# Causal mask added by TensorE for all 32 pairs of heads, in an attention plus SwiGLU kernel

## The chip, the cores and the metric

One NeuronCore of a Trainium2 chip runs the whole program. The metric is the device time of one execution, in microseconds (us); lower is better. PE is TensorE, DVE is VectorE, ACT is ScalarE, POOL is GpSimd, SP is SyncE, which here only issues DMAs.

## The reference, cut to what matters

```python
def _attn_ref(q, k, v, f):                       # q, k, v: 8 x 8 x 576 x 64; f: 8 x 8 x 576
    scores = scale * np.matmul(q, k.transpose(0, 1, 3, 2))
    cum = np.cumsum(np.log(np.clip(f, 0.0001, 1.0)), axis=-1)
    decay = cum[:, :, :, None] - cum[:, :, None, :]
    causal = np.triu(np.ones((S, S), dtype=bool), k=1)
    scores = np.where(causal, -1000000000.0, scores + decay)
    scores = scores - np.max(scores, axis=-1, keepdims=True)
    attn = np.exp(scores)
    attn = attn / (np.sum(attn, axis=-1, keepdims=True) + 1e-09)
    return np.matmul(attn, v)

def _moe_ref(x, w_gate, w_val, w_out):           # x: 4608 x 512; d_ff 1536
    g = x @ w_gate
    silu = g * (1.0 / (1.0 + np.exp(-g)))
    return silu * (x @ w_val) @ w_out
```

The attention output, with its heads side by side, is the input x of the second function. The gate sum of the query's own row drops out of the softmax, so the kernel needs only the sum of the key, as something that is added along a row of scores.

## The kernel before, in words

**Pairs.** Two heads make a pair p (0 to 31): 64 queries of one head and 64 of the other fill the 128 partitions. A pair has nine blocks of queries, i = 0 to 8, each with 64(i + 1) keys. They are worked in two units, g = 0 (blocks 0 to 3) and g = 1 (blocks 4 to 8), written a10.0, a10.1 and so on where the code names units.

**One unit.** `prepare` casts q and k to bf16 on POOL, transposes them on PE (L447) and copies them out (L459, L461). `scores` multiplies them on PE into a bank `sp` of PSUM (L493); there are two such banks for all pairs, and `BANKS` lists which blocks share one. DVE then adds the gate sums `cb` to the scores, writes the sum to a tile `t` in SBUF and takes the row's least value into a small tile `tm`, all in one instruction with a second one that stores the least value (L517, twice in the trace: a custom operation and a READ_ACCUMULATOR). The scores have their sign turned, so the least value is the softmax's maximum. ACT takes the exponential (L532), `normalize` makes the reciprocals of the row sums (`lr`, L546 to L550) and multiplies on POOL (L568); then P is transposed, on PE for pairs 0 to 7 (L598), by one DMA a pair for pairs 8 to 31 (L581). `weighted` multiplies P with v on PE (L624), and the result goes to `xT`, a ring of 2560 tokens (L648).

**The causal mask.** Only the last 64 keys of a block, its diagonal, need a mask. There are two ways, chosen by `MFROM = 12`. For pairs 0 to 11, PE adds the mask: a second matmul of 64 columns, identity times mask, accumulates into the diagonal's columns of the bank (L497). For pairs 12 to 31, `copies` makes a tile `cm` a pair, the gate sums with the mask added, on POOL or DVE (L476), and `scores` cuts the DVE instruction of a block in two: one for the keys before the diagonal, with `cb`, and one for the 64 of the diagonal, with `cm`. The second takes the least value of the first as its start:

```python
                if last and a < QB * i and p >= MFROM:
                    cuts += [(i, a, QB * i), (i, QB * i, z)]
```

**The feed-forward part.** `gate` and `project` work on tiles of 128 to 512 tokens: two matmuls to `gv` (L706), tanh on ACT (L712), two DVE products (L714, L717), then the output matmul (L734), a copy out (L741, L743) and a DMA (L746).

**The order.** Every operation is handed to a planner (`Plan`) with a cost for each engine that may do it, a latency `lat` after it, and a priority `prio`. The planner lays the operations out in time by these numbers, takes the one that can start earliest, and so fixes, before the program runs, which engine does what and in which order. Attention has the lower priority numbers and goes first; feed-forward work fills what is left. On the chip each engine runs its instructions in that fixed order and waits by semaphores. `NUDGE` is a list of additions to the priorities of single units (a: attention, f: gate, o: project, q: prepare); `HEAD` is the order of the units of pairs 0 to 3.

Of the kernel before, what the change touches and what calls it, by code (L numbers as in the profile page):

```python
# [8 lines left out]
F32 = mybir.dt.float32  # L9
BF16 = mybir.dt.bfloat16  # L10
AF = mybir.ActivationFunctionType
ALU = mybir.AluOpType
# [2 lines left out]
BIG = 1.0e9  # L15
HUGE = 3.0e38
COLD = 25000


class Op:  # L20
# [11 lines left out]
class Plan:  # L32
# [29 lines left out]
    def order(self):  # L62
# [72 lines left out]
        while ready:  # L135
            best = None
            for n, r in ready.items():
                o = self.ops[n]
                got = room(o, r)
                if got is None:  # L140
                    continue
                for e, dur in o.engs.items():
                    s = max(r, got[0], free[e])
                    for k in o.reads:
                        if k in using and using[k][0] != e:
                            s = max(s, using[k][1])
                    c = (s + o.bias.get(e, 0), o.prio, n, e, dur, got[1])
                    if best is None or c[:4] < best[:4]:
                        best = c
            if best is None:  # L150
                raise RuntimeError("no operation can start: " + ", ".join(str(self.ops[n].writes) for n in list(ready)[:20]))
            s, _, n, e, dur, take = best
            o = self.ops[n]
            s -= o.bias.get(e, 0)
            if e == "PE" and s < COLD:
                dur *= 2
            for k, b in take:
                name = self.home[k]
                self.where[k] = b
                slots[name][b] = k  # L160
                taken[name, self.line[k]] += 1
            o.start, o.eng = s, e
            free[e] = s + dur
            for k in o.reads:
                if self.home.get(k) in self.banks:
                    using[k] = e, s + dur + 30
            if o.dma:
                q = e == "POOL"
                at = max(wire[q], s + (2550 if q else 2000))
                both = max(0, min(2 * o.dma, wire[not q] - at))  # L170
                wire[q] = at + o.dma + both / 2
                wire[not q] += both / 2
                if o.ring:
                    free[e] = max(free[e], wire[q] - 1450)
                o.end = wire[q] + 1100
            else:
                o.end = free[e] + o.lat
            for k in {*o.writes, *o.reads, *o.holds}:
                left[k] -= 1
                until[k] = max(until[k], o.end)  # L180
            del ready[n]
            for kid in kids.get(n, ()):
                waiting[kid.n] -= 1
                if not waiting[kid.n]:
                    ready[kid.n] = max(d.end for d in kid.deps)
            done.append(o)
# [10 lines left out]
def kernel(  # L197
# [12 lines left out]
    B, H, S, D = q.shape  # L210
# [3 lines left out]
    P = 128  # L214
# [19 lines left out]
             [[(8, 0, 512)], [(8, 512, 576), (6, 0, 448)], [(7, 0, 512)], [(5, 0, 384)], [(4, 0, 320)]]]  # L234


    MFROM = 12
    CMENG = ("POOL", "DVE")

    ON_PE = {(p, g) for p in range(8) for g in range(2)}  # L240

    NDIRECT = 0
    NSEL = 1
    MOST = (("p", 1), ("o", 2), ("f", 3))
# [11 lines left out]
    HEAD = "10 00 20 30 11 01 31 21"  # L256


    NUDGE = "a21.0:1 a31.1:10 f5:1 f7:4.5 o8:2 q11:-2 q15:4 q24:2.5"

    WAIT = ""
    ORDER = [(int(u[0]), int(u[1])) for u in HEAD.split()]
# [32 lines left out]
    for i in range(0, NB, 2):  # L295
        bufs(f"e{i}", [P, QB * (i + 2)], F32, 2)
    bufs("eo", [P, 512], F32, 4)
    bufs("tm", [P, NB + 1], F32, 6)
    bufs("ls", [P, NB, 2], F32, 6)
    bufs("lr", [P, NB], F32, 6)  # L300
    both = {}
    for n in ("pk", "pT"):
        both[n] = [sb.tile([P, sum(NSL), P], BF16, name=f"{n}{x}") for x in range(2)]
# [114 lines left out]
    def prepare(p):  # L418
        s = first[p]
        for name in ("k", "q"):  # L420
# [4 lines left out]
            def cast(e, name=name, fk=fk, bk=bk, KR=KR):  # L425
# [5 lines left out]
                    eng[e].tensor_scalar(dst, src, -scale, 1.0, op0=ALU.mult, op1=ALU.mult)  # L431
                else:
                    eng[e].tensor_copy(dst, src)
            engs = {"POOL": 850}
            if p < NPB:
                engs = {"POOL": 850, "ACT": 850, "DVE": 500} if name == "k" else {"POOL": 1050, "ACT": 1050, "DVE": 680}
            o = pl.op(engs, cast, [fk], [bk], s - 1 + (name == "q") * .1)
# [30 lines left out]
    def copies(p):  # L468

        if p < MFROM:  # L470
            return
        pl.key(("cm", p), "cm")

        def add(e):
            src = pl.buf(("cb", p)).rearrange("r (i c) -> r i c", c=QB)
            eng[e].tensor_tensor(pl.buf(("cm", p)), src, maskf.unsqueeze(1).to_broadcast((P, NB, QB)), op=ALU.add)  # L476
        cost = {"POOL": S * 1.05 + 245, "DVE": S / .96 + 82}
        pl.op({e: cost[e] for e in CMENG}, add, [(("cb", p), 3)], [("cm", p)], first[p] - .5, holds=[("cb", p)])

    def scores(p, g):  # L480
        s = at[p, g]
        pl.key(("tm", p, g), "tm")
        pl.key(("ls", p, g), "ls")
        for n, bank in enumerate(BANKS[g]):
            sk = ("sp", p, g, n)
            pl.key(sk, "sp")
            pr = s + n * .05

            def mult(e, bank=bank, sk=sk):
                sp, kt, qz, o = pl.buf(sk), pl.buf(("kt", p)), pl.buf(("qz", p)), 0  # L490
                for i, a, z in bank:
                    last = z == QB * (i + 1)
                    nc.tensor.matmul(sp[:, o:o + z - a], qz[:, i, :, :].rearrange("p h r -> p (h r)"), kt[:, a:z],  # L493
                                     start=True, stop=not last or p >= MFROM)
                    o += z - a
                    if last and p < MFROM:
                        nc.tensor.matmul(sp[:, o - QB:o], ident, mask, start=False, stop=True)  # L497
            cols = [z - a for _, a, z in bank] + [64 for i, a, z in bank if z == QB * (i + 1) and p < MFROM]
            pl.op({"PE": mm(*cols)}, mult, [("kt", p), ("qz", p), (("kt", p), "done"), (("qz", p), "done"), "mask"], [sk], pr, lat=220)
            o = 0  # L500
            cuts = []
            for i, a, z in bank:
                last = z == QB * (i + 1)
                if last and a < QB * i and p >= MFROM:
                    cuts += [(i, a, QB * i), (i, QB * i, z)]
                else:
                    cuts.append((i, a, z))
            for i, a, z in cuts:
                last = z == QB * (i + 1)
                own = last and p >= MFROM  # L510
                tk = ("t", p, i)
                if a == 0:
                    pl.key(tk, "t")

                def add(e, i=i, a=a, z=z, o=o, sk=sk, tk=tk, last=last, own=own):
                    tm = pl.buf(("tm", p, g))
                    nc.vector.tensor_tensor_reduce(  # L517
                        out=pl.buf(tk)[:, a:z], in0=pl.buf(sk)[:, o:o + z - a],
                        in1=pl.buf(("cm", p))[:, i, :] if own else pl.buf(("cb", p))[:, a:z], scale=1.0,
                        scalar=HUGE if a == 0 else tm[:, NB:NB + 1], op0=ALU.add, op1=ALU.min,  # L520
                        accum_out=tm[:, i:i + 1] if last else tm[:, NB:NB + 1])
                w = [tk, ("tm", p, g)] + ([("m", p, i)] if last else [("m", p, i, "part")])
                r = [sk] + ([("cm", p)] if own else [(("cb", p), 3)]) + ([("m", p, i, "part")] if a else [])
                pl.op({"DVE": (z - a) / .96 + (142 if a else 82)}, add, r, w, pr, lat=100, holds=[] if own else [("cb", p)])
                o += z - a
                if last:
                    ek = ("e", p, i)
                    pl.key(ek, epool(i))

                    def exp(e, i=i, tk=tk, ek=ek):  # L530
                        L = QB * (i + 1)
                        nc.scalar.activation(pl.buf(ek)[:, :L], pl.buf(tk)[:, :L], AF.Exp,  # L532
                                             bias=pl.buf(("tm", p, g))[:, i:i + 1], scale=-1.0,
                                             accum_out=pl.buf(("ls", p, g))[:, i, 0:1])
                    sums[p, g] = pl.op({"ACT": QB * (i + 1) * .833 + 290}, exp, [tk, ("m", p, i)], [ek, ("ls", p, g)],
                          pr, lat=150, holds=[("tm", p, g)])

    def normalize(p, g):
# [10 lines left out]
        pl.op({"DVE": 95, "ACT": 200}, guard, [("ls", p, g)] + ([("z", "ls", n) for n in range(6)] if p < 3 else []), [("lr", p, g)], s, lat=120)  # L549
        pl.op({"DVE": 95}, lambda e: nc.vector.reciprocal(lr(), lr()), [("lr", p, g)], [("l2", p, g)], s, lat=170, holds=[("lr", p, g)])  # L550
        kk = ("pk", p, g)
        joint = not any((p, x) in ON_PE for x in range(2))
        pl.key(kk, f"pk{g}", same=("pk", p, 1 - g) if joint else None)
        w = HI[g] - LO[g] + 1
        for i in range(HI[g], LO[g] - 1, -1):
# [75 lines left out]
    def spread(p, g, pv):  # L631
# [5 lines left out]
        for a, z in ((0, cut), (cut, w)):  # L637
# [3 lines left out]
            def evac(e, a=a, z=z):  # L641
# [5 lines left out]
                src = bass.AP(src.tensor, src.offset + QB * (z - a - 1), [full[0], [-QB, z - a], full[2]])  # L647
                (nc.scalar.copy if e == "ACT" else nc.vector.tensor_copy)(dst, src)  # L648
            tok = t0 + a * QB, t0 + z * QB
            o = pl.op({"ACT": QB * (z - a) * .833 + 130, "DVE": QB * (z - a) / .96 + 85}, evac, [xk],  # L650
                      [("x", hp, n) for n in range(tok[0] // QB, tok[1] // QB)], s)
            o.bias = LATER if p >= 8 else {}
            evacs.append((pv, tok))
# [1 line left out]
    def load_v(b):  # L655
        for c in range(5):
# [9 lines left out]
                (), [fk], s, dma=1460 if n == P else 800, after=wait)  # L666
            def cast(e, c=c, n=n, fk=fk):
                (nc.scalar.copy if e == "ACT" else eng[e].tensor_copy)(pl.buf(("vt", b))[0:n, c, :, :], pl.buf(fk)[0:n, :, :])
            o = pl.op({"POOL": 670} if b else {"POOL": 670, "ACT": 580, "DVE": 600}, cast,
                  [fk] + ([("z", "vt", b)] if c == 4 and b < 2 else []), [("vt", b), ("vt", b, c)], s + .5)  # L670
            o.bias = SPARE

# [183 lines left out]
```

## Time and profile before

| | |
|---|---|
| median of 3 runs | 425.94 us (425.29 to 428.68) |
| the profiled execution | 422.99 us, span 421.1 us |
| busy: PE, DVE, ACT, POOL | 397.9, 349.9, 318.6, 269.3 us |
| instructions L497 (mask by PE) | 108 |
| instructions L517 (custom operations) | 460 |
| instructions L476 (`cm`) | 12 on DVE, 8 on POOL |

The span is the profiled execution from its first to its last instruction; its own time is 1.9 us longer. A busy share of PE counts records that overlap: matmuls are pipelined, and a record lasts longer than the time after which the next one starts.

### The profile page before, as it was taken

Reading aid. Unit: us, or ns where it says so; the run is one execution under the profiler, and the core shown is the slowest. Engines: PE = TensorE matmul, PEld = TensorE weight load, DVE = VectorE, ACT = ScalarE, POOL = GpSimd, SP = SyncE. Lnnn points to the kernel's source line nnn. Section 1 sums busy time; section 2 is a strip of 40 time slices with the busy share of each in tenths; the row PEclk is TensorE's granted clock in tenths of the full one; section 3 lists DMA queues with packets and bytes.
Section 4 is the critical chain, followed back from the end, with each engine's and each line's share of the span. In section 5 each row is a group of like instructions: output and inputs, shape, how many; then the busy total and the mean of one; then the engine's idle time right before and its main releaser. Section 6 shows DMA issues by size and latency. Waiting matters only on the chain.

```text
span 421.1 us, 10007 instructions
## 1 busy us (share of the span) xinstructions
PE 397.9 (94%) x3124; PEld 226.6 (54%) x3124; DVE 349.9 (83%) x1329; ACT 318.6 (76%) x882; POOL 269.3 (64%) x468
## 2 busy tenths in 40 slices
PE   2579999999999999999999999999999999999996
PEld 1446888665555555444544455454544444457675
DVE  4699999989998999899998999899989972765132
ACT  4599999999987989878998898798897843332221
POOL 7399978999985968767798696777964630000000
PEclk9999999999999999999999999999999999999999
DMA  7999999997999999999897999989948234000121
GB/s 199 197 151 248 213 213 208 230 233 181 203 205 198 262 189 225 225 247 190 175 228 187 235 208 214 221 193 188 224 113 166 57 85 115 2 25 27 51 76 50
DMA packets 143029, 72.21 MB, mean 171 GB/s; under 512 B 117760, under 2 KB 129792, under 8 KB 142976
## 3 DMA queue, kind: packets, MB, share of 16 engines
q1 hardware_dynamic: 136804, 66.27, 72.4%
q0 software_dynamic: 5808, 4.72, 7.5%
q10 hardware_dynamic: 364, 0.59, 0.5%
q8 instruction: 24, 0.39, 0.4%
q14 instruction: 29, 0.24, 0.2%
HBM read 47.04 MB, written 9.58 MB: 134 GB/s over the span
## 4 chain that ended last, share of the span: by engine, by line
PE 65%; DVE 18%; ACT 4%; issue 4%; DMA 4%; POOL 3%; SPq 0%; DVEq 0%; ACTq 0%; POOLq 0%
PE gv L706 33%; PE gv L734 16%; DVE t L517 10%; PE sp L493 7%; PE tx L624 4%; DMA qf<-in_q_dram 3%; DVE th L714 3%; PE tx L447 3%; DVE hh L717 3%; PE gv L598 2%; POOL pk L568 2%; ACT e L532 1%; ACT eo L532 1%; DVE qz L461 1%; DVE tm L517 1%
## 5 line engine op out<-in xcount | busy, mean ns | idle before, releaser
L568 POOL TENSOR_SCALAR pk<-e,lr 128x512 bf16<-128x512 f32 (+3 forms) x190 | 104.3, 552 | 55.6 <-issue 15.5
L517 DVE CUSTOM_DVE_ANT_0 t<-sp,cb 128x320 f32<-128x320 f32 (+7 forms) x268 | 121.0, 461 | 12.8 <-PE sp L493 1.7
L706 PE MATMUL gv<-xT,wv 128*128 128x512 bf16 (+2 forms) x576 | 111.2, 326 | 0.7 <-DVE th L714 0.6
L706 PE MATMUL gv<-xT,wg 128*128 128x512 bf16 (+2 forms) x576 | 111.4, 326 | 0.0
L734 PE MATMUL gv<-wo,hh 128*128 128x512 bf16 (+1 forms) x444 | 105.2, 373 | 0.0
L532 ACT ACTIVATE e<-t,tm 128x64 f32<-128x64 f32 (+4 forms) x160 | 88.6, 555 | 10.5 <-DVE tm L517 9.8
L714 DVE SCALAR_TENSOR_TENSOR th<-th,gv 128x512 f32<-128x512 f32 x108 | 73.8, 683 | 26.5 <-ACT th L712 25.8
L712 ACT ACTIVATE th<-gv 128x512 f32<-128x512 f32 x108 | 63.6, 590 | 32.5 <-PE gv L706 30.9
L532 ACT ACTIVATE eo<-t,tm 128x256 f32<-128x256 f32 (+3 forms) x128 | 71.3, 558 | 15.5 <-DVE tm L517 13.4
L493 PE MATMUL sp<-kt,qz 128*128 128x448 bf16 (+4 forms) x320 | 73.3, 293 | 6.6 <-DVE tm L517 5.8
L717 DVE TENSOR_TENSOR hh<-th,gv 128x512 bf16<-128x512 f32 x108 | 73.8, 684 | 4.2 <-PE gv L706 1.3
L568 POOL TENSOR_SCALAR pk<-eo,lr 128x256 bf16<-128x256 f32 (+3 forms) x128 | 68.2, 533 | 6.7 <-DVE tm L517 3.3
L706 PEld LDWEIGHTS <-wv 128*128 128x128 bf16 x576 | 50.6, 98 | 38.1 <-issue 3.6
L706 PEld LDWEIGHTS <-wg 128*128 128x128 bf16 x576 | 50.4, 98 | 36.8 <-issue 0.6
L734 PEld LDWEIGHTS <-hh 128*128 128x128 bf16 x444 | 41.0, 98 | 40.2 <-issue 1.0
L493 PEld LDWEIGHTS <-qz 128*128 128x128 bf16 x320 | 30.6, 100 | 27.3 <-issue 5.2
L517 DVE CUSTOM_DVE_ANT_0 t<-sp,cm,tm 128x64 f32<-128x64 f32 x160 | 42.2, 278 | 2.1 <-PE sp L493 0.2
L741 ACT ACTIVATE ot<-gv 128x512 f32<-128x512 f32 (+1 forms) x33 | 19.0, 578 | 25.5 <-PE gv L734 25.0
L517 DVE DVE_READ_ACCUMULATOR2_ANT tm<- 128x1 f32 x460 | 38.1, 83 | 0.0
L431 POOL TENSOR_SCALAR qb<-qf 72x1024 bf16<-72x1024 f32 x30 | 31.2, 1040 | 6.2 <-DMA qf<-in_q_dram 5.3
L459 ACT COPY qz<-tx 64x576 bf16<-64x576 bf16 x46 | 28.9, 628 | 3.5 <-PE tx L447 3.0
L532 ACT ACTIVATION_READ_ACCUMULATOR e<-t,tm 128x1 f32 x160 | 30.5, 191 | 0.0
(64 smaller groups left out, 403.1 us busy)
## 6 DMA issues: line engine op xcount, KB each, us to landing
out_dram<-ot SPq DMA_DIRECT2D x35, 256.0 KB
kf<-in_k_dram SPq DMA_DIRECT2D x31, 288.0 KB
qf<-in_q_dram SPq DMA_DIRECT2D x31, 288.0 KB
cb<-cum_f SPq DMA_DIRECT2D x62, 144.0 KB
vf<-in_v_dram SPq DMA_DIRECT2D x32, 256.0 KB
wo<-in_moe_w_out_dram POOLq DMA_DIRECT2D x3, 512.0 KB, 10.8
vf<-in_v_dram SPq DMA_DIRECT2D x8, 128.0 KB
wv<-in_moe_w_val_dram POOLq DMA_DIRECT2D x2, 512.0 KB, 7.6
```

The costliest lines, as they stand in the source:

```text
L431: eng[e].tensor_scalar(dst, src, -scale, 1.0, op0=ALU.mult, op1=ALU.mult)
L459: nc.scalar.copy(dst, src)
L493: nc.tensor.matmul(sp[:, o:o + z - a], qz[:, i, :, :].rearrange("p h r -> p (h r)"), kt[:, a:z], start=True, stop=not last or p >= MFROM)
L517: nc.vector.tensor_tensor_reduce(out=pl.buf(tk)[:, a:z], in0=pl.buf(sk)[:, o:o + z - a], in1=pl.buf(("cm", p))[:, i, :] if own else pl.buf ...
L532: nc.scalar.activation(pl.buf(ek)[:, :L], pl.buf(tk)[:, :L], AF.Exp, bias=pl.buf(("tm", p, g))[:, i:i + 1], scale=-1.0, accum_out=pl.buf(( ...
L568: eng[e].tensor_scalar(dst, src, r, 1.0, op0=ALU.mult, op1=ALU.mult)
L706: nc.tensor.matmul(pl.buf(bk)[:, j * n:j * n + n], wt[:, ko, fc * P:fc * P + P], xT[:, ko, x0:x0 + n], start=ko == 0, stop=ko == KD - 1)
L712: pl.op({"ACT": 487}, lambda e, u=u: nc.scalar.activation(pl.buf(("th", t, u)), pl.buf(("wg", t, u)), AF.Tanh, scale=0.5), [("wg", t, u)], ...
L714: pl.op({"DVE": 605}, lambda e, u=u: nc.vector.scalar_tensor_tensor(pl.buf(("th", t, u)), pl.buf(("th", t, u)), 1.0, pl.buf(("wg", t, u)), ...
L717: pl.op({"DVE": 605}, lambda e, u=u: nc.vector.tensor_mul(pl.buf(("hh", t, u)), pl.buf(("th", t, u)), pl.buf(("wv", t, u))), [("u", t, u), ...
L734: nc.tensor.matmul(pl.buf(bk)[:, 0:z - a], hh[:, (fc % nf) * n + ms * P:(fc % nf) * n + ms * P + P], wo[:, fc, a:z], start=fc == 0, stop=f ...
L741: nc.scalar.mul(pl.buf(ok)[:, a:z], pl.buf(bk)[:, 0:z - a], 0.5)
```

## The change

`MFROM` becomes 32, so PE adds the mask for every pair; no `cm` is made and no DVE instruction is cut. A second way for the cut blocks (`TWO`: both parts take their own least value and POOL joins them) comes with the diff, but `p >= MFROM` holds for no pair, so it makes no instruction. `JFROM = 8` names the pairs with one joint DMA transpose; they are the same pairs as before. `tm` gets another shape, `lr` has five buffers instead of six. The planner's numbers change: DVE costs 3% more after 100 us of planned time, the latency after L517 is 140 instead of 100 for pairs from 8 on, and the costs of the casts of q, k and v and of the copies to `xT` are others. `NUDGE` gets 18 more entries. `HEAD` stays.

```diff
+SLOW = 1.03
...
             if e == "PE" and s < COLD:
                 dur *= 2
+            if e == "DVE" and s > 100000:
+                dur *= SLOW
...
-    MFROM = 12
+    MFROM = 32
     CMENG = ("POOL", "DVE")
 
     ON_PE = {(p, g) for p in range(8) for g in range(2)}
 
+    JFROM = 8
+    TWO = True
...
-    NUDGE = "a21.0:1 a31.1:10 f5:1 f7:4.5 o8:2 q11:-2 q15:4 q24:2.5"
+    NUDGE = "a10.0:1 a13.0:2 a15.0:-1 a15.1:-0.5 a16.1:-2 a20.0:-1 a21.0:1 a23.1:-1 a26.1:0.5 a27.1:-1.5 a28.0:1 a29.0:1 a31.1:10 f3:-4 f4:-7 f5:1 f6:2 f7:4.5 f8:4 f9:8 o6:-2.5 o8:2 q11:-2 q15:4 q22:5.5 q24:2.5"
...
-    bufs("tm", [P, NB + 1], F32, 6)
+    bufs("tm", [P, 2, NB], F32, 6)
     bufs("ls", [P, NB, 2], F32, 6)
-    bufs("lr", [P, NB], F32, 6)
+    bufs("lr", [P, NB], F32, 5)
...
-            engs = {"POOL": 850}
+            engs = {"POOL": 850 if p < 8 else 800 if name == "k" else 1010}
...
-        cost = {"POOL": S * 1.05 + 245, "DVE": S / .96 + 82}
+        cost = {"POOL": 1350, "DVE": 710}
...
+                two = TWO and p >= MFROM and (not last or a > 0)
...
-                        scalar=HUGE if a == 0 else tm[:, NB:NB + 1], op0=ALU.add, op1=ALU.min,
-                        accum_out=tm[:, i:i + 1] if last else tm[:, NB:NB + 1])
+                        scalar=HUGE if a == 0 or two else tm[:, 1, i:i + 1], op0=ALU.add, op1=ALU.min,
+                        accum_out=tm[:, int(not last), i:i + 1])
...
-                pl.op({"DVE": (z - a) / .96 + (142 if a else 82)}, add, r, w, pr, lat=100, holds=[] if own else [("cb", p)])
+                pl.op({"DVE": (z - a) / .96 + (142 if a and not two else 82)}, add, r, w, pr, lat=100 if p < 8 else 140, holds=[] if own else [("cb", p)])
...
-        joint = not any((p, x) in ON_PE for x in range(2))
+        joint = p >= JFROM
...
-            o = pl.op({"ACT": QB * (z - a) * .833 + 130, "DVE": QB * (z - a) / .96 + 85}, evac, [xk],
+            o = pl.op({"ACT": QB * (z - a) * .833 + (130 if p < 8 else 50), "DVE": QB * (z - a) / .96 + 85}, evac, [xk],
...
-            o = pl.op({"POOL": 670} if b else {"POOL": 670, "ACT": 580, "DVE": 600}, cast,
+            o = pl.op({"POOL": 670 if b < 2 else 590} if b else {"POOL": 670, "ACT": 580, "DVE": 600}, cast,
```

More of the change, by code (lines that the diff above doesn't have):

```diff
@@ L513, in scores, with add @@
                     pl.key(tk, "t")
-                def add(e, i=i, a=a, z=z, o=o, sk=sk, tk=tk, last=last, own=own):
+                two = TWO and p >= MFROM and (not last or a > 0)
+                def add(e, i=i, a=a, z=z, o=o, sk=sk, tk=tk, last=last, own=own, two=two):
                     tm = pl.buf(("tm", p, g))
@@ L519, in add, with least @@
                         in1=pl.buf(("cm", p))[:, i, :] if own else pl.buf(("cb", p))[:, a:z], scale=1.0,
-                        scalar=HUGE if a == 0 else tm[:, NB:NB + 1], op0=ALU.add, op1=ALU.min,
-                        accum_out=tm[:, i:i + 1] if last else tm[:, NB:NB + 1])
-                w = [tk, ("tm", p, g)] + ([("m", p, i)] if last else [("m", p, i, "part")])
-                r = [sk] + ([("cm", p)] if own else [(("cb", p), 3)]) + ([("m", p, i, "part")] if a else [])
-                pl.op({"DVE": (z - a) / .96 + (142 if a else 82)}, add, r, w, pr, lat=100, holds=[] if own else [("cb", p)])
+                        scalar=HUGE if a == 0 or two else tm[:, 1, i:i + 1], op0=ALU.add, op1=ALU.min,
+                        accum_out=tm[:, int(not last), i:i + 1])
+                w = [tk, ("tm", p, g)] + ([("m", p, i, a)] if two else [("m", p, i)] if last else [("m", p, i, "part")])
+                r = [sk, ("cm", p) if own else (("cb", p), 3)] + ([("m", p, i, "part")] if a and not two else [])
+                pl.op({"DVE": (z - a) / .96 + (142 if a and not two else 82)}, add, r, w, pr, lat=100 if p < 8 else 140, holds=[] if own else [("cb", p)])
+                if last and two:
+                    def least(e, i=i):
+                        m = pl.buf(("tm", p, g))[:, :, i:i + 1]
+                        eng[e].tensor_scalar(m[:, 0, :], m[:, 1, :], m[:, 0, :], None, op0=ALU.min)
+                    pl.op({"POOL": 150}, least, [("m", p, i, 0), ("m", p, i, a)], [("m", p, i)], pr - .5, lat=120, holds=[("tm", p, g)])
                 o += z - a
@@ L532, in exp @@
                         nc.scalar.activation(pl.buf(ek)[:, :L], pl.buf(tk)[:, :L], AF.Exp,
-                                             bias=pl.buf(("tm", p, g))[:, i:i + 1], scale=-1.0,
+                                             bias=pl.buf(("tm", p, g))[:, 0, i:i + 1], scale=-1.0,
                                              accum_out=pl.buf(("ls", p, g))[:, i, 0:1])
```

## The prediction

> **What bounds the kernel now.** I read the page's busy row first, then busy time by stretches, then the PE groups by shape, the list of waits, and the timeline where PE waits. The stretches are cut where the work changes: to 119 us the scores belong to pairs 0 to 11 (the last L497 record starts at 118.8), to 345 us to pairs 12 to 31, and behind that only the feed-forward part is left.
>
> ```profile
> 50.00:119.00 69.00, 68.86 (x709) 46.20 (x707) 66.69 (x237) 67.33 (x190) 62.04 (x103) 1.00 1.03 212
> 119.00:169.00 50.00, 49.52 (x369) 25.21 (x367) 47.28 (x198) 43.53 (x126) 37.86 (x62) 1.00 1.05 214
> 169.00:219.00 50.00, 49.20 (x337) 24.30 (x336) 46.36 (x216) 42.98 (x123) 38.48 (x63) 1.00 0.99 213
> 219.00:269.00 50.00, 48.49 (x345) 24.38 (x344) 46.67 (x201) 42.86 (x125) 40.35 (x66) 1.00 1.01 212
> 269.00:345.00 76.00, 74.72 (x483) 36.29 (x482) 70.56 (x303) 61.58 (x181) 50.95 (x87) 1.00 0.69 151
> 345.00:421.10 76.10, 72.87 (x550) 44.59 (x547) 33.72 (x50) 21.92 (x38) 0.00 (x0) 1.00 0.17 53
> ```
>
> The columns are stretch, length, then busy us of PE, weight loads, DVE, ACT and POOL, granted clock, DMA share and GB/s. PE is nearly full everywhere and the clock is 1.00; DVE is at 93 to 97% until 345 us and then falls away, while PE has 76 us of feed-forward work left. So PE sets the end: what PE works more, or waits less, moves the end by as much, and what the other engines save counts only where PE waits for them.
>
> A busy PE is not a PE at its peak. A 512-column record lasts 379 ns, but in an undisturbed row of matmuls the next starts 216 ns later. I therefore took the start of every matmul from the trace and subtracted the undisturbed spacing of its shape (216 ns at 512 columns, 109 at 256, 56 at 128, 28.5 at 64). That gives some 373 us of PE work and 37 us lost up to the last matmul's start; the first 50 us lose 17 of it. From 119 to 345 us, counting losses over 40 ns each, there are 10.7 us that end with a release by another engine: 8.3 us before L493, on a bank `sp` that DVE still reads, 1.3 before L706, 1.1 before L447. Another 7.6 us are some 106 losses of about 72 ns at L624, with nothing released near them; a change of shape and column group goes with them, and I leave them alone. From 50 to 119 us the first kind makes 0.8 us.
>
> **The change, part by part.**
>
> *Matmuls added.* Nine a pair (108 records for 12 pairs), 20 pairs more: 180. Their price is the spacing in the stretch that has them.
>
> ```profile
> 108.66 0.27 PE L493 MATMUL sp<-kt,qz 128*128 128x256 bf16 x1
> 108.77 0.19 PE L497 MATMUL sp<-mask,ident 128*128 128x64 bf16 x1
> 108.80 0.25 PE L493 MATMUL sp<-kt,qz 128*128 128x192 bf16 x1
> 108.89 0.19 PE L497 MATMUL sp<-mask,ident 128*128 128x64 bf16 x1
> 108.91 0.19 PE L493 MATMUL sp<-kt,qz 128*128 128x64 bf16 x1
> 108.94 0.19 PE L497 MATMUL sp<-mask,ident 128*128 128x64 bf16 x1
> 108.97 1.03 PE L706 MATMUL gv<-xT,wg 128*128 128x512 bf16 x4
> ```
>
> The record is 0.19 us long, but the next matmul starts 28 or 29 ns after it: 180 x 28.5 ns = **+5.1 us**, all on PE's path. Bounds: 28 ns, 5.0 us; 53 ns, the upper quartile over all 108, which counts the half-filled first 50 us, 9.5 us. I take the steady value.
>
> *Weight loads.* Each added matmul brings a load of `ident`:
>
> ```profile
> L497 PEld LDWEIGHTS <-ident x108: 95/98/147, 13.0 to 118.8; 128*128 128x128 bf16 x108
> ```
>
> A load of 98 ns stands beside a matmul of 28 ns, yet starts stay 28 ns apart, so loads hide. If that cover were gone: 180 x 98 ns = 17.6 us. The Trainium skill speaks against the change here: its page "TensorE: Matmul & The Clock Gate", section "LDWEIGHTS (loading the stationary operand)", gives a load P/1.2 ns, 107 ns for 128 columns, and the section "Back-to-back issue gap" says that the spacing of load and matmul pairs is set by both, some 81 ns at 128 columns. By 107 ns a pair the 180 would cost an estimated 19 us. The timeline above differs from that rule, with 28 ns.
>
> *DVE work removed.* Seven blocks a pair were cut, so 17 L517 operations become 10: 140 fewer. The second part costs 203 ns from its start to the next start (mean), and the uncut instruction is longer by 64 columns, 66 ns (681 - 617, 553 - 485): 140 x 137 ns = 19.2 us. `cm` on DVE: 12 x 0.78 us start to start = 9.4 us. DVE is thus freed of some 28 of its 211 us between 119 and 345 us, 93% becoming about 81%. `cm` on POOL: 8 x 1.41 us = 11.3 us. None of this is on PE's path by itself; what counts is how early DVE frees a bank:
>
> ```profile
> 234.28 0.48 DVE L517 CUSTOM_DVE_ANT_0 t<-sp,cb 128x320 f32<-128x320 f32 x1
> 234.69 0.08 DVE L517 DVE_READ_ACCUMULATOR2_ANT tm<- 128x1 f32 x1
> 234.69 0.68 DVE L717 TENSOR_TENSOR hh<-th,gv 128x512 bf16<-128x512 f32 x1
> 235.29 0.28 DVE L517 CUSTOM_DVE_ANT_0 t<-sp,cm,tm 128x64 f32<-128x64 f32 x1
> 235.50 0.09 DVE L517 DVE_READ_ACCUMULATOR2_ANT tm<- 128x1 f32 x1
> ```
> ```profile
> 234.32 1.04 PE L706 MATMUL gv<-xT,wg 128*128 128x512 bf16 x4
> 235.64 0.38 PE L493 MATMUL sp<-kt,qz 128*128 128x256 bf16 x3 [0.28 <-DVE tm L517]
> ```
>
> Here a block of 384 keys is cut in 320 and 64, and a feed-forward product of 0.6 us runs between the parts. PE's four matmuls are through at 234.32 + 4 x 0.216 = 235.18; the bank comes free at 235.59; PE starts at 235.64 and has lost 0.46 us. Uncut, the operation takes 0.48 us start to start and its READ_ACCUMULATOR 0.08: the bank is free at 234.85, before PE wants it. The Trainium skill has a rule the other way: "Perfetto Trace Analysis", section "Optimizing Scalar/DVE Operations", says that breaking up instructions may end bubbles on other engines. This row shows the opposite, because a bank is free only after both parts.
>
> *Waits that go.* The list of PE's waits has, from 119 to 345 us,
>
> ```profile
> PE sp L493 <- DVE tm L517: 2.0, 8, 0.4
> PE gv L706 <- DVE th L714: 0.6, 2, 0.3
> ```
>
> and from 50 to 119 us no entry, though DVE is 97% busy there. (It counts only idle time between records, so it shows a part of my 10.7 us.) At the rate of 50 to 119 us, 0.8 us in 69, the 226 us would keep 2.6; at DVE's lower load I take 2.0. The bounds are 0 and 10.7. So **-8.7 us**.
>
> *The planner's numbers, NUDGE, `lr`, `tm`.* They remove no instruction. The old numbers are off where the new ones come nearer: q casts planned at 850 and taking 1040 ns, `cm` on POOL planned at 850 and taking 1409. What another order is worth no row shows; I bound it by the waits, from none to the rate of the worst stretch, 200 to 250 us, where the first kind made 3.3 us: 14.9 us over the 226, 4.2 above today's. I take nothing beyond the waits above. With five `lr`, a unit's first write would wait for the fifth unit before; the nearest such POOL work ended 8.4 us earlier, so it costs nothing. Were that cover gone, L714 and the next L517 would queue behind it on DVE. No DMA is added; SP's transposes (L581), which wait for POOL, may issue earlier. If attention then runs ahead, the 76 us of feed-forward work at the end covers it: PE stays fed.
>
> *Sum.* +5.1 - 8.7 = **-3.6 us** on the profiled execution's 422.99 us, so 419.4. The median of the runs shown lies 2.95 us above that execution; I put the same difference on it: 425.94 - 3.6 = **422.3 us**.
>
> **The rivals.**
>
> *The waits stay (slower).* Place: PE's queue at L493. The order is fixed beforehand, and PE would meet a busy bank as often as now, because planned and real times still part and feed-forward products still run between bank reads. Price: +5.1 if all 10.7 us stay (431.0), +9.3 at the worst stretch's rate (435.2). It decides from 10.7 - 5.1 = 5.6 us of waits left; above 9.9 left the loss is over 1%. For it: the worst waits have a 0.6 us product in between. Against: the stretch with PE masks has almost none under as full a DVE. Chance 0.23, 0.13 of it beyond 1%.
>
> *More goes than I count.* All 10.7 us and a part of the 7.6 at L624, should the new order change what stands before L624: -5.6 to -9, some 419. Against: those losses occur in every stretch, with either mask. Chance 0.17.
>
> *It does nothing.* Freed DVE time is filled with copies that ACT did, attention runs denser, and new waits at `tx` and `gv` eat the gain: between -1 and +2, some 426.5. Today L706 and L447 wait only 2.4 us. Chance 0.06.
>
> *Loads are not hidden.* +17.6 less 5.1 to 8.7 for waits, some 436. The timeline denies it. Chance 0.02.
>
> **How the numbers follow.** The forecast, -1.1 to -5.1 (4.5 us of waits left to 0.5), has 0.52; about 0.16 of that lies beyond 1%, with under 1.3 us of waits left. About 1% is what a measurement of this kernel can tell from no change. Faster: 0.16 + 0.17 = 0.33. Slower: 0.13 + 0.02 = 0.15. The rest, 0.52, is the same. The range reaches from all waits gone and 2.3 us more (-7.9, 418.0) to 9.2 us of waits left (+3.6, 429.5); some 0.2 lies outside. The forecast's own range is 420.8 to 424.8.
>
> **What would show it.** Right: L497 x288, 320 L517 operations, no L476; the added matmuls spaced 28 to 29 ns; DVE near 81% from 119 us to the end of attention; attention ending before 340 us with a longer pure feed-forward end; PE's waits on `tm` nearly gone. Wrong: PE losing more than 5 us on releases behind 119 us, mask matmuls 50 ns or more apart, or new waits before L624, L706 or L447 as large as those that went.

## The result, and the profile after

The changed kernel takes 421.09 us (median of 14 runs) where the kernel before takes 425.86 us (14 runs): ratio 0.9883, 95% interval 0.9856 to 0.991, 4.8 us less. The forecast was 422.3 us, within 418.0 to 429.5. The gain is 1.2%, a little over the 1% that the prediction took as the least that a measurement of this kernel can tell from no change. The profiled execution took 420.02 us, its span is 418.2 us.

The stretches of the kernel after, with the columns of those shown before (busy us of PE, weight loads, DVE, ACT, POOL, then clock, DMA share and GB/s):

```profile
119.00:169.00 50.00, 50.00 (x403) 26.34 (x400) 44.04 (x150) 44.82 (x136) 36.47 (x66) 1.00 1.08 219
169.00:219.00 50.00, 49.90 (x405) 26.49 (x404) 44.94 (x157) 43.96 (x133) 40.23 (x71) 1.00 1.04 217
219.00:269.00 50.00, 49.69 (x395) 26.22 (x394) 42.55 (x150) 42.36 (x128) 38.30 (x66) 1.00 1.11 228
269.00:345.00 76.00, 75.93 (x533) 38.09 (x531) 57.23 (x181) 54.27 (x156) 38.78 (x72) 1.00 0.71 147
345.00:418.20 73.20, 70.00 (x526) 43.22 (x524) 32.38 (x48) 20.96 (x36) 0.00 (x0) 1.00 0.12 44
```

PE is full where it had gaps of 0.5 to 1.5 us a stretch. Attention is also done earlier: PE starts the last matmul of a score (L498, L493 before) at 314.7 us instead of 336.7, so the rest is feed-forward work alone, for longer.

The list of what PE waited for between 119 and 345 us has one line left:

```profile
PE tx L638 <- DMA pT<-pk: 0.3, 1, 0.3
```

The wait of L493 (L498 in the new file) on `tm` is gone from it. A bank in the timeline of PE, with the added matmuls (L502):

```profile
202.31 0.27 PE L498 MATMUL sp<-kt,qz 128*128 128x256 bf16 x1
202.42 0.19 PE L502 MATMUL sp<-mask,ident 128*128 128x64 bf16 x1
202.45 0.25 PE L498 MATMUL sp<-kt,qz 128*128 128x192 bf16 x1
202.53 0.19 PE L502 MATMUL sp<-mask,ident 128*128 128x64 bf16 x1
202.56 0.19 PE L498 MATMUL sp<-kt,qz 128*128 128x64 bf16 x1
202.59 0.19 PE L502 MATMUL sp<-mask,ident 128*128 128x64 bf16 x1
```

From the start of each matmul, as in the prediction, up to the last one's start:

| | before | after | difference | forecast |
|---|---|---|---|---|
| PE's work by undisturbed spacing | 372.8 us | 378.0 us | +5.2 | +5.1 |
| lost between matmuls | 37.1 us | 28.3 us | -8.8 | -8.7 |
| of it ended by another engine's release, 119 to 345 us | 10.7 us | 1.0 us | -9.7 | -8.7 |
| first to last matmul | 409.8 us | 406.2 us | -3.6 | -3.6 |
| first matmul | 7.8 us | 8.5 us | +0.7 | |

The first matmul came 0.7 us later in this execution, so the spans differ by 2.9 us. The medians differ by 4.8: the profiled execution of the kernel before lies 2.9 us under its median, that of the kernel after 1.1 us under its own. That the traces differ by the forecast's 3.6 us to a tenth is therefore in part luck.

### The profile page after: what moved, and what is told of

Same layout as the page of the kernel before. It is cut to its first block, busy times and chain, and to the rows that moved or that the text cites. A ratio compares the mean times of both kernels' runs of the same rounds, so it can differ in the third digit from the quotient of the medians.

```text
span 418.2 us, 9999 instructions
## 1 busy us (share of the span) xinstructions
PE 398.1 (95%) x3304; PEld 231.8 (55%) x3304; DVE 325.3 (78%) x1044; ACT 311.0 (74%) x875; POOL 252.6 (60%) x460
## 4 chain that ended last, share of the span: by engine, by line
PE 77%; DMA 7%; ACT 6%; POOL 4%; DVE 3%; issue 2%; SPq 0%; POOLq 0%; DVEq 0%; ACTq 0%
PE gv L720 38%; PE gv L748 20%; PE sp L498 8%; PE tx L638 5%; DMA kf<-in_k_dram 3%; PE tx L452 3%; POOL pk L582 3%; PE gv L612 2%; DMA pT<-pk 2%; DVE t L526 2%; ACT eo L546 2%; ACT e L546 2%; PE sp L502 1%; DMA cb<-cum_f 1%; DMA cum_f<-t 1%
## 5 line engine op out<-in xcount | busy, mean ns | idle before, releaser
L526 DVE CUSTOM_DVE_ANT_0 t<-sp,cb 128x512 f32<-128x512 f32 (+7 forms) x288 | 130.9, 475 | 13.5 <-PE sp L502 5.0
L582 POOL TENSOR_SCALAR pk<-e,lr 128x128 bf16<-128x128 f32 (+3 forms) x190 | 100.1, 530 | 32.7 <-DVE lr L564 15.1
L748 PE MATMUL gv<-wo,hh 128*128 128x512 bf16 (+1 forms) x444 | 107.5, 374 | 0.0
L546 ACT ACTIVATE e<-t,tm 128x448 f32<-128x448 f32 (+4 forms) x160 | 88.5, 555 | 4.6 <-DVE tm L526 3.9
L498 PE MATMUL sp<-kt,qz 128*128 128x448 bf16 (+6 forms) x320 | 72.8, 295 | 3.8 <-DVE tm L526 3.7
L720 PEld LDWEIGHTS <-wv 128*128 128x128 bf16 x576 | 49.3, 98 | 34.8
L748 PEld LDWEIGHTS <-hh 128*128 128x128 bf16 x444 | 39.7, 98 | 37.1
L502 PE MATMUL sp<-mask,ident 128*128 128x64 bf16 x288 | 48.2, 197 | 0.0
L498 PEld LDWEIGHTS <-qz 128*128 128x128 bf16 x320 | 31.0, 101 | 19.8 <-DVE qz L466 1.3
L502 PEld LDWEIGHTS <-ident 128*128 128x128 bf16 x288 | 27.2, 100 | 15.2 <-issue 3.9
L638 PE MATMUL tx<-pT,vt 128*64 128x320 bf16 (+4 forms) x448 | 29.4, 266 | 0.7 <-DMA pT<-pk 0.3
```

Source lines behind the costliest of these rows:

```text
L526: nc.vector.tensor_tensor_reduce(out=pl.buf(tk)[:, a:z], in0=pl.buf(sk)[:, o:o + z - a], in1=pl.buf(("cm", p))[:, i, :] if own else pl.buf ...
L582: eng[e].tensor_scalar(dst, src, r, 1.0, op0=ALU.mult, op1=ALU.mult)
L638: nc.tensor.matmul(xo[r, 0:QB * n], vt[:, c, 2 * hp + h, :], pT[:, a:a + n, 64 * h:64 * h + 64], start=(c == 0), stop=(c == nch - 1))
L720: nc.tensor.matmul(pl.buf(bk)[:, j * n:j * n + n], wt[:, ko, fc * P:fc * P + P], xT[:, ko, x0:x0 + n], start=ko == 0, stop=ko == KD - 1)
L748: nc.tensor.matmul(pl.buf(bk)[:, 0:z - a], hh[:, (fc % nf) * n + ms * P:(fc % nf) * n + ms * P + P], wo[:, fc, a:z], start=fc == 0, stop=f ...
```

## The experiments

All ratios are to the kernel before, run on the same chip in the same batch (medians 425.6 to 427.1 us). "Numbers" means the planner's costs and latency, as against NUDGE. Where a run is set against the changed kernel, its ratio is compared with 0.9883, which was measured in another batch. The five buffers of `lr` and the new shape of `tm` were not tried apart.

**1. The mask alone.**

```diff
 (the kernel before)
-    MFROM = 12
+    MFROM = 32
```

> The kernel before with MFROM = 32 alone: PE masks for all pairs, no cm, no cut, but the old planner numbers, the old NUDGE, six lr buffers. Theory 1 (the cut and cm make the waits, so removing them is enough): 180 matmuls add 5.1 us, releases by DVE on sp fall from 8.3 us to about 2, so some 2 to 4 us below the kernel before, ratio 0.990 to 0.995. Theory 2 (the waits go because the planner's numbers and NUDGE changed): the waits stay and the added matmuls show, 3 to 6 us above, ratio 1.007 to 1.014.

Measured: 425.92 us, ratio 0.9985 (0.9949 to 1.0022). Neither theory: the waits on `sp` went, but the gain did not come. What PE waits for from 119 to 345 us:

```profile
PE tx L447 <- POOL kb L433: 1.5, 2, 1.2
PE tx L624 <- DMA pT<-pk: 1.4, 1, 1.4
PE tx L447 <- POOL qb L431: 1.1, 1, 1.1
```

No line has `tm`: the losses at L493 that end with a release by DVE are down from 8.3 us to under 1. But PE now comes to the transposes of q and k (L447) before POOL has cast them, and to one `weighted` before its P has come. The waits moved.

**2. The order without the mask.**

```diff
 (the changed kernel)
-    MFROM = 32
+    MFROM = 12
-    TWO = True
+    TWO = False
```

> The changed kernel with MFROM = 12 and TWO = False: cm and the cut come back for pairs 12 to 31, while the new planner numbers, the new NUDGE and five lr buffers stay. Theory 1: 5.2 us less PE work, but the waits on sp come back, so within 1% of the kernel before, ratio 0.993 to 1.007. Theory 2: the waits stay gone without the added matmuls, 5 to 9 us below the kernel before, ratio 0.979 to 0.988.

Measured: 439.57 us, ratio 1.0300 (1.0246 to 1.0354), which neither theory had. Some 14 us of PE's losses behind 119 us end with DVE freeing a bank. That is not all of it. The columns of this row are those of the stretches above, the third from the end is PE's granted clock:

```profile
169.00:219.00 50.00, 43.32 (x284) 21.68 (x288) 40.62 (x183) 37.83 (x110) 32.17 (x54) 0.90 0.95 203
```

In this execution PE's clock was granted at half for 20.5 us in three pieces (10.2, 3.4 and 6.8 us), in which matmuls of 512 columns start 427 ns apart instead of 216. PE lost some 10.2 us by that, of the 16.9 us by which the span (438.0 us) exceeds that of the kernel before. Over their whole spans all six runs had a mean clock of 0.977 to 0.981, where the profiled executions of the kernels before and after had 1.000.

**3. and 4. The changed kernel with the NUDGE of before, and with the numbers of before.** The edits put back the lines that the diff shows.

> The changed kernel with the NUDGE of before; masks on PE and the new planner numbers stay. Theory 1: NUDGE is worth little, 0 to 2 us above the changed kernel (421 to 423). Theory 2, in the form that NUDGE took the waits away: 4 us or more above it (425 or more), with over 5 us of PE's losses between 119 us and the end of attention ended by another engine's release.

> The changed kernel with the planner numbers of before (no 3% on DVE, latency 100 after the DVE add, old costs of casts and copies); masks on PE and the new NUDGE stay. Theory 1: 0 to 2 us above the changed kernel (421 to 423). Theory 2, in the form that the nearer planner numbers took the waits away: 4 us or more above it, with PE waits on sp back at 5 us or more behind 119 us.

Measured: 421.87 us, ratio 0.9875 (0.9816 to 0.9935) with the old NUDGE, 424.60 us, 0.9952 (0.9909 to 0.9995) with the old numbers. The 18 new entries of NUDGE are worth nothing that these runs can tell (0.9875 against 0.9883); the numbers are worth some 0.7% by experiment 4, whose interval just touches that of the change, or 1.1% if experiment 1 is compared with experiment 3. The profiled execution of experiment 4 was the fastest of its twelve (420.51 us, span 418.7), so its trace does not show what the old numbers cost.

**5. and 6. The mask with one half of the numbers each.** Both start from experiment 1.

```diff
 (5: costs of casts and copies)
-            engs = {"POOL": 850}
+            engs = {"POOL": 850 if p < 8 else 800 if name == "k" else 1010}
...
 (6: costs of DVE)
+            if e == "DVE" and s > 100000:
+                dur *= 1.03
...
-                pl.op({"DVE": ...}, add, r, w, pr, lat=100, ...
+                pl.op({"DVE": ...}, add, r, w, pr, lat=100 if p < 8 else 140, ...
```

> The kernel before with MFROM = 32 and the new planner costs of the casts of q, k and v and of the copies to xT; NUDGE, the DVE numbers and lr stay as before. With the mask alone PE no longer waited on sp, but waited 3.4 us for the casts of q and k on POOL and 1.4 us for a P transpose. Theory A (the planner's cast costs, 850 ns for a q cast that takes 1040, put PE's transposes too early): these waits fall to under 1 us and the ratio to before becomes 0.986 to 0.992. Theory B (the DVE numbers, 3% and latency 140, are what counts): it stays at 0.996 to 1.001, as with the mask alone.

> The kernel before with MFROM = 32 and the new DVE numbers of the planner (3% more after 100 us, latency 140 after L517 from pair 8 on); casts, NUDGE and lr as before. Theory A: no better than the mask alone, 0.996 to 1.001, with PE still waiting over 2 us for POOL's casts from 50 to 345 us. Theory B: 0.986 to 0.992.

Measured: 0.9949 (0.9903 to 0.9994) with the cast costs, 0.9943 (0.9905 to 0.9981) with the DVE costs. Theories A and B both fall as they were forecast. By the medians each half gives part of it, but the intervals tell the halves apart neither from each other nor from the mask alone (0.9949 to 1.0022). With the cast costs alone PE still waits 1.9 us for two casts of k.

**7. The price of the added matmuls.**

```diff
 (the changed kernel)
-                        nc.tensor.matmul(sp[:, o - QB:o], ident, mask, start=False, stop=True)
+                        nc.tensor.matmul(sp[:, o - QB:o], ident, mask, start=False, stop=p < 12)
+                        if p >= 12:
+                            nc.tensor.matmul(sp[:, o - QB:o], ident, mask, start=False, stop=True)
```

> The changed kernel with the mask matmul of pairs 12 to 31 made twice (the second adds the same mask again, which changes nothing after the exponential); the planner is not told, so the order is the same. If PE sets the end, 180 more matmuls of 28.5 ns cost 5.1 us: ratio to the changed kernel 1.012 (426 where it is 421), bounds 4 to 7 us. If PE had slack that the added matmuls of the change fell into: under 1.5 us. If the loads of ident come to show when two stand in a row: 12 us or more.

Measured: 426.67 us, ratio 1.0024 (0.9989 to 1.0059); against the changed kernel's 0.9883 that is +1.4%, about 6 us, give or take 2. PE's work rose by 5.2 us (383.2 against 378.0). A timeline row of it:

```profile
202.18 0.19 PE L502 MATMUL sp<-mask,ident 128*128 128x64 bf16 x1
202.21 0.19 PE L504 MATMUL sp<-mask,ident 128*128 128x64 bf16 x1
202.24 0.25 PE L498 MATMUL sp<-kt,qz 128*128 128x192 bf16 x1
```

PE sets the end, and a mask matmul costs 29 ns (median of the 180) whether or not another stands before it.

**8. and 9. The cut alone, and `cm` alone, put back.**

```diff
 (8: the changed kernel, both parts with cb)
-                if last and a < QB * i and p >= MFROM:
+                if last and a < QB * i and p >= 12:
 (9: the changed kernel, cm made and not read)
-        if p < MFROM:
+        if p < 12:
             return
         pl.key(("cm", p), "cm")
```

> The changed kernel with the seven blocks of pairs 12 to 31 cut again, both parts with cb, as two planned operations between which other work may stand; masks stay on PE, no cm. DVE gets 140 x 137 ns = 19.2 us back, and the planner knows of it. If the cut is what made PE wait on sp: over 5 us of such waits behind 119 us and 3 to 8 us above the changed kernel, ratio to before 0.996 to 1.008. If cm was the cause: within 2 us of the changed kernel, 0.985 to 0.993.

> The changed kernel with the 20 cm tiles still made on POOL or DVE, as planned operations that nothing reads; no cut, masks on PE. DVE and POOL together get some 21 us back. If cm was a cause of the waits: 3 us or more above the changed kernel, ratio to before 0.996 or more, with PE waiting for POOL's casts or P. If only the cut was: within 2 us of the changed kernel, 0.985 to 0.993.

Measured: 432.92 us, 1.0130 (1.0066 to 1.0193) with the cut, 429.45 us, 1.0058 (1.0012 to 1.0103) with `cm`. Either alone takes time, about 2.5% and 1.8% above the changed kernel. In the two profiles PE waits on `tm` again (2.5 us and 1.6 us of idle time from 119 to 345 us), which is less than the 5 us that was expected of the cut.

The 2.5% is not the price of those waits alone. In the profile of the cut PE's clock was at half for two pieces of 6.8 us, and the 6.8 us that PE lost by it are half of the 13.8 us by which the span exceeds the changed kernel's (432.0 against 418.2). One of the two pieces begins at 44 us, before any block is cut; PE had waited 1.5 us for a cast of v there. All six runs had a mean clock of 0.984 to 0.992. With `cm` the profiled execution had the full clock.

**10. The cut, with nothing between the parts.** The operation of a block makes both DVE instructions, one right behind the other; the planner sees one operation at its old cost.

```diff
 (the changed kernel, pairs 12 to 31)
+                    if last and a < QB * i and p >= 12:
+                        m = QB * i
+                        nc.vector.tensor_tensor_reduce(out=pl.buf(tk)[:, a:m], ..., scalar=HUGE, accum_out=tm[:, 1, i:i + 1])
+                        nc.vector.tensor_tensor_reduce(out=pl.buf(tk)[:, m:z], ..., scalar=tm[:, 1, i:i + 1], accum_out=tm[:, 0, i:i + 1])
+                        return
```

> The changed kernel, but for pairs 12 to 31 each of the 7 blocks is again done by two DVE instructions, back to back inside one planned operation, both with cb; the planner's order is that of the changed kernel, and nothing can come between the two. DVE gets 140 x 137 ns = 19.2 us back. If what made the waits was the 0.6 us product between the parts, the loss stays small: 0 to 2 us above the changed kernel (421 to 423), PE's waits on sp under 2 us. If it was DVE's load as such: 4 us or more above it (425 or more).

Measured: 436.70 us, ratio 1.0233 (1.0174 to 1.0292). So 15 us above the changed kernel, at a clock of 1.000 in the profile. This is no clean test of the product between the parts. The second part takes its start from the first one's READ_ACCUMULATOR, and back to back that costs 119 ns from start to start which the planned order filled with other work: a block of 384 keys takes 410 + 119 + 209 = 738 ns instead of 477, so DVE got some 140 x 260 ns = 36 us back, not 19.2. PE's losses on `sp` came back at 14.4 us, in more than one place:

```profile
PE sp L498 <- DVE tm L533: 3.4, 13, 0.6
PE sp L498 <- DVE tm L539: 2.1, 6, 0.9
```

**11. DVE work that touches no bank.**

```diff
 (the changed kernel, behind the add of each block that was cut, pairs 12 to 31)
+                    if last and a < QB * i and p >= 12:
+                        nc.vector.tensor_tensor(pl.pools["cm"][0][:, 0, :], maskf, maskf, op=ALU.add)
```

> The changed kernel with one more 128x64 addition on DVE, written to a tile that nobody reads, behind each of the 140 operations that were cut before; the planner is not told, so the order is that of the changed kernel. It adds some 140 x 0.14 to 0.2 us = 20 to 28 us to DVE between 119 and 345 us and lets every bank free as early as before. If DVE has slack there (81% by my sum), PE waits under 3 us more and the time is 0 to 3 us above the changed kernel. If an order made for a lighter DVE can't bear it: waits on sp come back as in the kernel with the joined cut (14 us), 6 us or more above.

Measured: 444.70 us, ratio 1.0437 (1.0388 to 1.0487), 5.6% or some 24 us above the changed kernel. Stretches and waits of this kernel:

```profile
119.00:169.00 50.00, 45.46 (x352) 24.11 (x357) 46.64 (x154) 40.56 (x119) 33.22 (x59) 0.97 0.89 194
169.00:219.00 50.00, 46.45 (x358) 24.39 (x364) 49.43 (x176) 39.28 (x123) 35.84 (x63) 1.00 0.96 202
...
PE sp L498 <- DVE tm L526: 11.5, 16, 2.3
```

DVE is nearly full, PE is not, and PE's losses on `sp` are some 18 us. But the dose is not what was meant. Half of the 140 additions take 150 ns or less from start to start; the mean is 337 ns, 47 us in all instead of 20 to 28:

```profile
L532 DVE TENSOR_TENSOR cm<-maskf 128x64 f32<-128x64 f32 x140 | 56.1, 401 | 0.0
...
185.91 2.94 DVE L532 TENSOR_TENSOR cm<-maskf 128x64 f32<-128x64 f32 x1
186.94 0.82 POOL L438 CAST kb<-kf 96x768 bf16<-96x768 f32 x1
187.74 1.04 POOL L436 TENSOR_SCALAR qb<-qf 72x1024 bf16<-72x1024 f32 x1
188.77 0.48 DVE L526 CUSTOM_DVE_ANT_0 t<-sp,cb 128x320 f32<-128x320 f32 x1
189.31 0.22 PE L498 MATMUL sp<-kt,qz 128*128 128x128 bf16 x1 [2.33 <-DVE tm L526]
```

The addition reads two tiles in SBUF. Here it ends 0.08 us behind the second cast on POOL, 2.9 us after its start, and PE waits 2.3 us for the bank behind it. Of the 140, 50 take more than 300 ns; every one of them starts while POOL works and ends 64 to 182 ns after a POOL instruction has ended. So the additions waited for POOL, and PE's three largest losses on `sp` (1.7 to 2.5 us) stand behind additions of 1.9 to 2.9 us.

What is left of the test: the additions hold no bank, and they delay only what stands behind them in DVE's queue, the next block of the same bank among it. DVE work that the order did not foresee thus makes PE wait, by some 24 us for 47 us, 1.7 us of it by half clock. What 21 us would have cost is not shown, and neither is what made PE wait in the kernel before, whose order was made with the cut.

That question the trace of before answers in part. Of its 38 losses over 40 ns before L493 that end with a release by DVE, 12 have a product, a copy or the making of `cm`, each of 0.6 us or more, directly before the part that frees the bank; they hold about 40% of the time lost. In the others parts of blocks, or the short operations for `lr`, follow one another. The product of the prediction's timeline was one of several ways in which a bank came late.

**12. The numbers alone.** The kernel before with all new planner numbers, those for `cm` included, and nothing else.

> The kernel before with all the new planner numbers and nothing else: cm and the cut stay for pairs 12 to 31, NUDGE, lr and tm stay. If the numbers help by themselves: 0.985 to 0.995. If they help only where the mask is on PE: 0.997 to 1.005. If they are what made the mixed kernel (new numbers and NUDGE with cm and the cut) 3% slower: 1.02 or more, with over 10 us of PE's waits on sp.

Measured: 441.07 us, ratio 1.0335 (1.0285 to 1.0384). PE's waits from 119 to 345 us, then one stretch of it, then the second of the waits counted from 50 to 400 us:

```profile
PE sp L495 <- DVE tm L519: 5.2, 7, 1.3
PE tx L626 <- DMA pT<-pk: 0.7, 1, 0.7
...
169.00:219.00 50.00, 44.65 (x293) 22.48 (x298) 46.20 (x205) 41.93 (x124) 36.45 (x61) 0.93 0.97 193
...
PE tx L626 <- DMA pT<-pk: 5.9, 2, 5.2
```

The P transposes thus cost PE one wait of 5.2 us more, behind 345 us. Here too PE's clock was at half, for 17.1 us in three pieces, and PE lost some 8.5 us by it, of the 18.1 us by which the span (439.2 us) exceeds that of before. All six runs had a mean clock of 0.977 to 0.981. In experiments 2, 8, 11 and 12 each piece at half clock begins 1 to 3.1 us after the start of an idle spell of PE of 0.9 us or more. Not every such spell is followed by one: with `cm` kept, spells of 1.8 and 1.6 us were not. So a wait of PE can cost more than its own length, and which ones do these runs don't tell.

With experiments 1 and 3 this makes a table of two by two, all with the old NUDGE (experiment 3 has five `lr` and the new `tm` besides):

| ratio to before | old numbers | new numbers |
|---|---|---|
| `cm` and cut, pairs 12 to 31 | 1 | 1.0335 |
| mask on PE for all | 0.9985 | 0.9875 |

The two parts of the change are worth nothing, or harm, one by one; together they give the gain. With the new NUDGE, the mask and the old numbers give 0.9952 (experiment 4). About half of the harm in the upper right is PE's clock. Why the new numbers bring the waits that go with it was not tried apart; the latency of 140 ns between the two parts of a block, which pushes more foreign work between them, is a guess.

None of the kernels beats the changed one by more than its interval.

## Why the prediction was right, and where not

**The added matmuls: right.** 5.1 us forecast, 5.2 in the trace, about 6 in the doubled run. The stretch with masks showed the price of a whole bank in a row, so nothing had to be guessed. The weight loads stay hidden. The section "LDWEIGHTS (loading the stationary operand)" of the Trainium skill's page "TensorE: Matmul & The Clock Gate" would have a load take 107 ns; the records take 98 ns, and with two mask matmuls in a row starts are 29 ns apart, so the rival of open loads is out.

**The waits that go: right in size, in part by luck.** 8.7 us forecast, 8.8 lost less. My residual of 2.0 us was 1.0. The stretch of the first pairs was a good model of the changed kernel: same engines, same banks, mask on PE. But it was used to say what the mask alone does, and experiment 1 shows that there other waits take the place of those that go.

**The wait's cause: half right.** That a bank is late while DVE still has to free it holds. I had the cut delay a bank by the product in between, and the trace of before has other work of that size there in 12 of 38 losses. I also took DVE's freed time as worth nothing by itself ("None of this is on PE's path by itself"). Experiments 10 and 11 show otherwise: with a fixed order some 36 us more on DVE cost 15 us, and 47 us cost 24 us, 1.7 us of it by half clock. So 0.4 to 0.5 of what DVE gets beyond the plan reaches the end, though DVE has some 13% idle time in the changed kernel (170.7 us busy of the 195.7 from 119 us to the last score). I forecast 81% where it is 87%, mostly because I left attention's pace as it was: over the whole execution DVE's busy time fell by 24.6 us (349.9 to 325.3; some 28 forecast), but attention now ends 22 us earlier. Over the same 226 us it is 84%.

**The planner's numbers: the step that failed.** "I take nothing beyond the waits above" treated the numbers as free. The sum came out right because the change has both parts; that was luck. With the old numbers and the old NUDGE the same removal gives 0.15%, and the waits come up at L447 and L624 instead; the numbers are worth 0.7% to 1.1%, some 3 to 5 us. The run of the mask alone is the third rival, new waits that eat the gain, at a chance of 0.06. The trace of before had a possible hint, casts planned at 850 ns and taking 1040; but with the cast costs alone PE still waited for casts, so which of the numbers counts stays open.

**The rule on breaking up instructions.** "Optimizing Scalar/DVE Operations" of the page "Perfetto Trace Analysis" of the Trainium skill was set against one row here. The rule speaks of an engine that is not saturated; DVE was busy 93% of the time from 119 to 345 us in the kernel before, so this case does not refute it. Cutting the blocks again (experiment 8) costs about 2.5%, about half of it by PE's clock.

## What to carry to other kernels

Take the engine that sets the end by the spacing of its starts, not by its busy share, and sum what it works more against what it waits less; a stretch of the same kernel that already runs the new way gives both prices. Where an order is fixed beforehand by planned costs, work that the plan doesn't know can make another engine wait, even on an engine with 13% idle time. An edit and the costs that describe it must be tried together: alone, the edit here gave 0.15% and the costs lost 3.4%. Read PE's granted clock before you put a loss down to waits, and read the mean and the longest of what you added, not only its median: the dose of experiment 11 was twice what was meant.

## What the runs showed of the hardware that was not expected

Two matmuls of 64 columns with the same weights, each with its own load of 98 ns, still start 29 ns apart (experiment 7). A DVE add that takes a scalar from the READ_ACCUMULATOR just before it starts 119 ns behind that record's start (experiment 10), where what has no such tie mostly starts at the same time as that record (median 0 ns in the changed kernel). A DVE addition of two SBUF tiles that takes 0.22 us when it need not wait took up to 2.9 us while POOL worked (experiment 11). PE's clock was granted at half for pieces of 3.4 to 10.2 us, with 427 ns instead of 216 between matmuls of 512 columns (experiments 2, 8, 11 and 12).
